# Strassen sums of an attention kernel moved to another place in VectorE's order

## The chip, the cores and the metric

The kernel runs on one core of a Trainium2 chip. A core has five engines that work side by side, each with its own queue of instructions taken in order: TensorE (PE, matmul), VectorE (DVE), ScalarE (ACT), GpSimd (POOL) and SyncE (SP), which here only issues DMAs. An instruction waits in its queue until the semaphores it needs have their values. The metric is the device time of one execution in microseconds (us). The kernel before has a median of 1221.35 us over 3 runs (1220.94 to 1221.71).

## The reference

Cut to what matters; x is 2048 x 512, 32 heads of width 128, a cache of 2048 keys and values per head, everything in bf16.

```python
xn = layernorm(x)
q  = heads(xn @ wq)                                  # wq 512 x 4096
p  = softmax(einsum("bhqd,bhkd->bhqk", q, k_cache) * Dh ** -0.5)
o  = einsum("bhqk,bhkd->bhqd", p, v_cache)
s  = merge(o) @ wo                                   # wo 4096 x 512
# the gate: a small MLP mixer of xn
h  = gelu(layernorm(xn) @ w1); h = shift_tokens(h)   # four column groups, by -1, +1, -2, +2
x1 = xn + h @ w2
g  = silu(x1 + gelu(layernorm(x1) @ w3) @ w4)
return x + s * g
```

## The kernel before, in words

**Units and slots.** The gate is computed first (about the first 190 us, overlapping the first attention units) and stored to DRAM. Attention is cut into 128 units: 8 groups of 4 heads (g), in each group 4 quarters of 512 tokens (qt), in each quarter the 4 heads (hh). So a group is 16 units. A unit has 8 slots, and the main loop runs over `n`, with `u, p = divmod(n, 8)`. In each slot TensorE computes scores of 256 keys by 512 tokens into PSUM (ps_s), ACT takes their exp into an SBUF tile (pT, L446, 128x1024), and TensorE multiplies the exp tiles of an earlier slot with the values (ps_o). Four pT tiles of 128x2048 make a unit.

**Softmax sums.** The exp tiles of a unit are added up into one tile, acc: `add_first` on DVE (L452, pT0 + pT1, recorded in slot 4), then pT2, whose lower half POOL adds and whose upper half DVE adds (`add_half`, L457, both 128x1024), then pT3 (`add_next`, L461), then two folds (L465, L469) down to 128x512. A DMA transposes it (tT), DVE reduces it (L499) and takes the reciprocal (L505), two DMAs spread it over the partitions (dr, rb), and `norm` (L523) multiplies ps_o with rb into oT.

**The q product.** For each pair of heads, q of 512 tokens is computed by a Strassen scheme with seven half-size products in place of eight. It needs sums of blocks of xn (`x_sum`, tiles xs, L366: four per quarter of tokens, made once) and of blocks of wq (`w_sum`, tiles wc, L375: four per pair of heads). The products' results are put together by ACT (`q_take`, L415) and DVE (`q_part`, L423, L426, L428, L431). The last of these additions, L431 (`qT<-ps_q,tq`, 128x512), is recorded in slot 6 of an odd unit, and the scores of the next unit, an even one, read what it writes.

**The wo product.** The same scheme for o @ wo, per group and quarter: sums of blocks of wo (`wo_sum`, tiles tw, L563, four per group; the third of most groups overwrites a block of wo itself), sums of blocks of oT (`o_sum`, tiles so, L572, four per quarter), seven products for each of two row blocks, and `wo_take` (L597), which adds the results into fp32 accumulators in SBUF (sacc). At the end the accumulators are joined, scaled by the gate and added to x.

**What sets the order.** Everything is written out by hand: dictionaries from a slot number to operations. `todo` (filled by `at`) runs at the end of a slot. `o_early` runs in slot 0, and in slot 4 just ahead of `add_first`. `o_steps` runs at the end of a slot, behind `q_part` of the same slot and ahead of `add_half`. As each engine takes its instructions in the order in which they are recorded, this fixes DVE's order. In an odd unit the order is: what `o_early` holds for slot 4, L452, L431, then L523, L499, L505, an L597, DVE's L457, L461 and the folds.

**Memory.** Pool `pS` (right side) opens when the gate's tiles are done and lies over their memory; it holds xs, wc, tw, so, sacc and others. Pool `pB` lies on the left side; `qtp` is a ring of 5 tiles for the queries of the first units, otherwise unused later on. A tile that lies over memory that was in use waits for the last instructions or DMAs that used it. The first tile of sacc is cleared in unit 8 by a memset on DVE (L545); the gate stores are DMAs on POOL's queue (L321).

Of the kernel before, what the change touches and what calls it, by code (L numbers as in the profile page):

```python
# [11 lines left out]
BF16 = mybir.dt.bfloat16  # L12
# [5 lines left out]
def kernel(  # L18
# [16 lines left out]
    P = nc.NUM_PARTITIONS  # L35
# [9 lines left out]
    QT = Sq // 512  # L45
# [5 lines left out]
    HG = 4  # L51
    NG = H // HG

    SPU = KC // 2
# [9 lines left out]
    def pool(name, bufs=1, space=None, **kw):  # L64
        if space is not None:
            kw["space"] = space
        return tc.tile_pool(name=name, bufs=bufs, **kw)
# [43 lines left out]
    def mm(out, lhsT, rhs, start, stop, **kw):  # L111
# [9 lines left out]
        out=ident[:], in0=diag[:], scalar1=0.0, scalar2=None, op0=ALU.is_equal))  # L121

    HEAD = 7
    XS = 3 * QT + 1
    TW = (2, 1, 0, 1)
    units = [(g, qt, hh) for g in range(NG) for qt in range(QT) for hh in range(HG)]
    LATE = (QT - 2, QT - 1)
# [7 lines left out]
    def at(n, fn):  # L135
        todo[n].append(fn)
# [209 lines left out]
    xs = {}  # L346
# [4 lines left out]
    def x_block(qt, half, dcs):  # L351
        c = qt * 512 + 256 * half
        return xnT[:, dcs, c:c + 256]

    def x_sum(qt, i):
        if i == 2 and qt < QT - 1:
            out = x_block(qt, 1, LO)
        else:
            out = pS.tile([P, 2, 256], BF16, tag="xs", bufs=XS, name="xs")[:]
        a, b, op = (  # L360
            (x_block(qt, 1, LO), x_block(qt, 1, HI), ALU.add),
            (xs.get((qt, 0)), x_block(qt, 0, LO), ALU.subtract),
            (x_block(qt, 0, LO), x_block(qt, 1, LO), ALU.subtract),
            (x_block(qt, 0, HI), xs.get((qt, 1)), ALU.subtract),
        )[i]
        pin(nc.vector.tensor_tensor(out=out, in0=a, in1=b, op=op))  # L366
        xs[qt, i] = out
# [185 lines left out]
    def wo_sum(g, i):  # L553
        w = wog[g]
        b11, b12, b21, b22 = (w[:, k, c] for k in (UP, DOWN) for c in (WL, WR))
        if i == 2 and g < NG - 2:
            out = b12
        elif i == 2:
            out = qtp.tile([P, 2, D // 2], BF16, tag="qT", bufs=5, name="tw")[:]
        else:  # L560
            out = pS.tile([P, 2, D // 2], BF16, tag=f"tw{i}", bufs=TW[i], name="tw")[:]
        a, b = ((b12, b11), (b22, tw.get((g, 0))), (b22, b12), (b21, tw.get((g, 1))))[i]
        pin(nc.vector.tensor_tensor(out=out, in0=a, in1=b, op=ALU.subtract))  # L563
        tw[g, i] = out
# [173 lines left out]
    def last_act(ts, cols):  # L738
        tb[ts, cols.start] = pS.tile([P, D // 2], BF16, tag="xs", bufs=XS, name="tb")
        pin(nc.scalar.activation(  # L740
            out=tb[ts, cols.start][:], in_=last_ps(ts, cols), func=ACT.Identity, scale=0.5))
# [245 lines left out]
    pB = left.enter_context(pool("pB", reuse_waits="tile"))  # L987
# [3 lines left out]
    pS = None  # L991
    for h in range(HG):
        load_wo(h)
    for g in range(NG - 1):
        b = (g * QT + QT - 1) * HG
        for hh in range(HG):
            h = (g + 1) * HG + hh
# [74 lines left out]
    o_steps, o_early = defaultdict(list), defaultdict(list)  # L1072
    for g, qt in BLOCK:
        u0 = ((g * QT + qt) * HG + 6) * SPU
        for i in range(2):
            a = u0 + 16 * i
            for k, n in ((1, 10), (7, 11), (2, 14), (4, 15), (6, 19), (5, 20), (3, 23)):
                steps[a + n].append((wo_product, g, qt, i, k))
            for k, n, which in ((7, 12, o_early), (4, 16, o_early), (5, 22, o_steps), (3, 24, o_early)):
                which[a + n].append((wo_take, g, qt, i, k))  # L1080
        for i, n, which in ((2, 3, o_steps), (0, 4, o_early), (1, 12, o_early), (3, 19, o_steps)):
            which[u0 + n].append((o_sum, g, qt, i))
    for g in range(NG - 1):
        u0 = ((g * QT + (g == 0)) * HG + 6) * SPU
        for i, n in ((0, -4), (2, -4 if g else 4), (1, 4), (3, 12)):
            o_early[u0 + n].append((wo_sum, g, i))
    for i, (qt, u) in enumerate((qt, qt * HG + 5 + j) for qt in range(1, QT) for j in range(2)):
        at(u * SPU + 6, lambda qt=qt, i=i: sa_clear(qt, i % 2))
    LATER = (BLOCK[-1][0] * QT + BLOCK[-1][1] + 1) * HG
# [2 lines left out]
    for i, u in enumerate((10, 11, 12, 13, 14, 16, 18, 20)):  # L1092
        n = (LATER + u) * SPU
# [24 lines left out]
        for fn, *args in plan.get(n, ()):  # L1118
            fn(*args)

    for j, u in enumerate((8, 8, 9, 9, 9, 9, 9, 11, 11, 13, 17, 17, 18, 19, 20, 20)):
        at(u * SPU + 3, lambda qt=(j // 4 - 1) % QT, i=j % 4: x_sum(qt, i))
    for h in range(2, H, 2):
        for i, u in enumerate((((-4, -3, -3, -3), (-1, -1, 0, 0))[h % HG // 2] if h >= HG else (8, 8, 9, 9))):
            o_early[(h // HG * QT * HG + u) * SPU + 4].append((w_sum, h, i))

    for v in range(1, NU):
        if v not in made and not FIRST <= v < LAST + 2:
# [3 lines left out]
    for n in range(UB * SPU):  # L1132
        u, p = divmod(n, SPU)
# [73 lines left out]
        if pS is None and not held:  # L1207
            right.close()
            pS = right.enter_context(pool("pS", side="right", reuse_waits="tile"))
# [3 lines left out]
    n = UB * SPU  # L1213
# [15 lines left out]
    def last_add(ts, cols, tm):  # L1229
        if cols.start == 0:  # L1230
            yl[ts] = pS.tile([P, D], BF16, tag="xs", bufs=XS, name="y")
        pin(nc.vector.tensor_tensor(out=yl[ts][:, cols], in0=tm, in1=sacc[t0 + ts][:, cols.start // (D // 2)], op=ALU.add))  # L1232
# [8 lines left out]
    def pv_to(k):  # L1241
# [29 lines left out]
        out=diag[:], in0=diag[:], scalar1=0.0, scalar2=None, op0=ALU.is_equal))  # L1271
# [98 lines left out]
```

## Time and profile before

| what | value |
|---|---|
| median of 3 runs | 1221.35 us |
| the profiled execution | 1223.05 us |
| its span | 1221.3 us |
| PE busy | 1215.1 us, 99% |
| DVE busy | 1090.0 us, 89% |
| ACT busy | 1107.5 us, 91% |
| POOL busy | 299.2 us, 24% |
| granted TensorE clock | full in all slices |

The profile is of one execution on the chip. Busy time counts instructions on an engine's datapath. A line such as `L457 POOL ... x117 | 248.7, 2125 | 725.8 <-DVE acc L452 403.1` is a group of instructions of one line of the kernel: 117 of them, 248.7 us in all, 2125 ns each in the mean, and POOL sat idle 725.8 us before them, 403.1 of it ended by DVE's L452. A timeline row gives the start, the duration and the operation, and in brackets the engine's idle time before it and what ended it. `out<-in` are the program's names for the tiles. Rows of instructions that follow one another on one engine overlap by some hundredths of a microsecond, since the next starts while the last is still draining.

### The profile page before, as it was taken

The page shows a single profiled execution, that of the slowest core. Times are in us where ns is not written, and L with a number is a line of the kernel's source. Part 1 is how long each engine was busy: PE and PEld are TensorE (multiplying, and loading weights), DVE is VectorE, ACT ScalarE, POOL GpSimd, SP SyncE. Part 2 cuts the span into 40 slices and gives each one's busy share as a digit, 9 for nine tenths or more (in the row PEclk, how much of TensorE's full clock was granted, in tenths as well). Part 3 has the DMA queues.
Part 4 walks back from the last instruction along what each step waited for, and adds up shares of the span by engine and source line. Part 5 has one row for each costly group of instructions (what it writes and reads, how often), then busy time and mean ns, then how long its engine had stood idle before and what let it go on. Part 6 is the DMA issues. An engine that isn't in the chain of part 4 may idle for free.

```text
span 1221.3 us, 18941 instructions
## 1 busy us (share of the span) xinstructions
PE 1215.1 (99%) x6657; PEld 673.7 (55%) x6657; DVE 1090.0 (89%) x1931; ACT 1107.5 (91%) x1243; POOL 299.2 (24%) x222
## 2 busy tenths in 40 slices
PE   9999999999999999999999999999999999999998
PEld 6466444555555555555555555555555555555555
DVE  7763779999999999999999899999999999989997
ACT  6345999999999999999999999999999999999996
POOL 5300001323222222222222222222222222233320
PEclk9999999999999999999999999999999999999999
DMA  7662323444444434445343433344434434356552
GB/s 178 167 153 61 57 57 83 96 88 95 74 90 89 100 65 91 84 99 89 70 95 86 102 69 85 90 96 78 85 85 91 100 66 93 86 102 109 123 113 66
DMA packets 248159, 113.07 MB, mean 93 GB/s; under 512 B 195328, under 2 KB 231296, under 8 KB 248064
## 3 DMA queue, kind: packets, MB, share of 16 engines
q1 hardware_dynamic: 244560, 107.21, 41.4%
q0 software_dynamic: 2944, 4.20, 1.5%
q8 instruction: 52, 0.85, 0.3%
q14 instruction: 43, 0.35, 0.2%
q10 hardware_dynamic: 560, 0.46, 0.1%
HBM read 69.60 MB, written 4.45 MB: 61 GB/s over the span
## 4 chain that ended last, share of the span: by engine, by line
PE 96%; DVE 2%; ACT 1%; DMA 0%; issue 0%; DVEq 0%; ACTq 0%
PE ps_s L112 40%; PE ps_o L112 37%; PE ps_q L112 8%; PE ps_wo L112 8%; PE ps_m L112 3%; ACT pT L446 1%; DVE acc L461 0%; PE ps_warm L112 0%; DMA tT<-acc 0%; DVE acc L452 0%; DVE sacc L597 0%; PE ps_oh L112 0%; DVE y L1232 0%; DVE sm L499 0%; DVE acc L457 0%
## 5 line engine op out<-in xcount | busy, mean ns | idle before, releaser
L446 ACT ACTIVATE pT<-ps_s 128x1024 bf16<-128x1024 f32 x1016 | 1016.6, 1028 | 44.6 <-PE ps_s L112 12.8
L112 PE MATMUL ps_s<-qT,kT 128*128 128x512 bf16 (+1 forms) x2064 | 609.2, 377 | 1.5 <-ACT pT L446 0.9
L112 PE MATMUL ps_o<-pT,vb 128*128 128x512 bf16 x1984 | 589.9, 379 | 0.0
L457 POOL TENSOR_TENSOR acc<-acc,pT 128x1024 bf16<-128x1024 bf16 x117 | 248.7, 2125 | 725.8 <-DVE acc L452 403.1
L112 PEld LDWEIGHTS <-vb 128*128 128x128 bf16 x1984 | 194.0, 98 | 216.6
L112 PEld LDWEIGHTS <-kT 128*128 128x128 bf16 x2064 | 230.8, 113 | 73.7 <-DVE qT L431 3.0
L461 DVE TENSOR_TENSOR acc<-acc,pT 128x2048 bf16<-128x2048 bf16 x137 | 167.7, 1224 | 20.9 <-ACT pT L446 5.1
L452 DVE TENSOR_TENSOR acc<-pT 128x2048 bf16<-128x2048 bf16 x127 | 154.8, 1219 | 11.3 <-ACT pT L446 11.3
L597 DVE TENSOR_TENSOR sacc<-ps_wo,sacc 128x512 f32<-128x512 f32 x200 | 121.8, 609 | 3.0 <-PE ps_wo L112 1.7
L523 DVE TENSOR_TENSOR oT<-ps_o,rb 128x512 bf16<-128x512 f32 x127 | 86.6, 682 | 7.3 <-DMA rb<-dr 7.1
L465 DVE TENSOR_TENSOR acc<-acc 128x1024 bf16<-128x1024 bf16 x127 | 87.3, 687 | 2.4
L499 DVE TENSOR_REDUCE sm<-tT 128x4 f32<-128x512 bf16 x124 | 83.9, 677 | 5.8 <-DMA tT<-acc 5.5
L457 DVE TENSOR_TENSOR acc<-acc,pT 128x1024 bf16<-128x1024 bf16 x117 | 80.6, 688 | 0.0
L112 PEld LDWEIGHTS <-wc 128*128 128x128 bf16 x448 | 43.8, 98 | 52.9 <-issue 0.2
L112 PE MATMUL ps_wo<-wo_h,oT 128*128 128x256 bf16 (+1 forms) x296 | 71.1, 307 | 0.0
L112 PEld LDWEIGHTS <-oT 128*128 128x128 bf16 x428 | 41.6, 98 | 45.6
L112 PEld LDWEIGHTS <-so 128*128 128x128 bf16 x400 | 39.1, 98 | 47.2
L112 PEld LDWEIGHTS <-wq_h 128*128 128x128 bf16 x396 | 38.7, 98 | 46.1
L112 PE MATMUL ps_q<-xnT,wq_h 128*128 128x256 bf16 (+1 forms) x284 | 58.8, 295 | 0.0
L301 ACT ACTIVATE h2T<-ps_s 128x1024 bf16<-128x1024 f32 x28 | 28.6, 1023 | 31.6 <-PE ps_s L112 31.6
L469 DVE TENSOR_TENSOR acc<-acc 128x512 bf16<-128x512 bf16 x127 | 53.4, 420 | 2.4
L112 PEld LDWEIGHTS <-w_sb 128*128 128x128 bf16 x368 | 33.6, 98 | 29.2 <-issue 0.2
(134 smaller groups left out, 926.4 us busy)
## 6 DMA issues: line engine op xcount, KB each, us to landing
rb<-dr SPq DMA_DIRECT2D x127, 256.0 KB, 3.9
vb<-in_A_v_cache_dram SPq DMA_DIRECT2D x62, 256.0 KB, 3.0
wq_h<-in_A_wq_dram SPq DMA_DIRECT2D x32, 128.0 KB, 2.5
wo_h<-in_A_wo_dram SPq DMA_DIRECT2D x32, 128.0 KB, 2.4
w_sb<-in_B_w_dram SPq DMA_DIRECT2D x8, 256.0 KB, 5.0
kT<-in_A_k_cache_dram SPq DMA_TRANSPOSE x128, 2.7
gate<-xall POOLq DMA_DIRECT2D x16, 128.0 KB, 2.2
sacc<-in_A_x_dram POOLq DMA_DIRECT2D x8, 256.0 KB, 4.6
```

The costliest lines, as they stand in the source:

```text
L112: pin(nc.tensor.matmul(out=out, lhsT=lhsT, rhs=rhs, start=start, stop=stop, **kw))
L301: pin(nc.scalar.activation(out=h2[c][:, f], in_=ps[:], func=ACT.Gelu_apprx_tanh))
L446: pin(nc.scalar.activation(out=s["pT"][-1][:, jj:jj + 2, :], in_=sps[:], func=ACT.Exp, scale=SCALE))
L452: pin(nc.vector.tensor_tensor(out=s["acc"][:], in0=s["pT"][0][:], in1=s["pT"][1][:], op=ALU.add))
L457: pin(eng.tensor_tensor(out=a[:, part, :], in0=a[:, part, :], in1=e[:, part, :], op=ALU.add))
L461: pin(nc.vector.tensor_tensor(out=a[:], in0=a[:], in1=st[u]["pT"][i][:], op=ALU.add))
L465: pin(nc.vector.tensor_tensor(out=a[:, 0:2, :], in0=a[:, 0:2, :], in1=a[:, 2:4, :], op=ALU.add))
L469: pin(nc.vector.tensor_tensor(out=a[:, 0, :], in0=a[:, 0, :], in1=a[:, 1, :], op=ALU.add))
L499: pin(nc.vector.tensor_reduce(out=sm[:], in_=s["tT"][:], axis=mybir.AxisListType.X, op=ALU.add))
L523: pin(nc.vector.tensor_tensor(out=to, in0=o, in1=rb, op=ALU.mult))
L597: pin(nc.vector.tensor_tensor(out=out, in0=ps, in1=out, op=ALU.add))
```

## The change

It touches where sums of the two Strassen schemes are recorded, and in which pool a few of their tiles lie. The number of operations is the same (1526 tensor-tensor operations on DVE), and the orders on TensorE, ACT, POOL and SP are the same; only DVE's order differs.

- **Token sums (`x_sum`).** The sixteen move from units 8 to 20 to units 2 to 11. Tiles of the quarters 0 and 3 come from the left pool (tag "xe", 7 tiles), those of quarters 1 and 2 from pS as before (6 instead of 13 tiles).
- **`o_sum` number 1** moves from slot 4 of an odd unit, ahead of L452, to slot 6 of that unit, behind L431.
- **Weight sums of wo (`wo_sum`).** From group 1 on, numbers 1 and 3 take their tiles from the ring `qtp`, and the four are spread over three or four units; those in odd units stand in slot 6, behind L431, those in even units in slot 4, ahead of L452.
- **Weight sums of wq (`w_sum`).** From head 4 on, spread over units -4, -4, -3, -3 or -2, -1, 0, 0 before their group; those in odd units stand in slot 6, behind L431.

In the new DVE order 49 of the 56 L431 have one to three of these sums directly behind them; before, none had.

```diff
-    XS = 3 * QT + 1
+    XE, XS = 7, 3 * (QT - 2)
...
-            out = pS.tile([P, 2, 256], BF16, tag="xs", bufs=XS, name="xs")[:]
+            pl, tag, n = (pS, "xs", XS) if 0 < qt < QT - 1 else (pB, "xe", XE)
+            out = pl.tile([P, 2, 256], BF16, tag=tag, bufs=n, name="xs")[:]
...
-        elif i == 2:
+        elif i == 2 or i % 2 and g:
             out = qtp.tile([P, 2, D // 2], BF16, tag="qT", bufs=5, name="tw")[:]
...
-        for i, n, which in ((2, 3, o_steps), (0, 4, o_early), (1, 12, o_early), (3, 19, o_steps)):
+        for i, n, which in ((2, 3, o_steps), (0, 4, o_early), (1, 14, o_steps), (3, 19, o_steps)):
             which[u0 + n].append((o_sum, g, qt, i))
+    WSUMS = [[(i, 8 * u + (4, 6)[u % 2]) for i, u in us] for us in (
+        ((0, -5), (1, -3), (2, -2), (3, -1)), ((0, -13), (1, -5), (2, -2), (3, -1)))]
     for g in range(NG - 1):
         u0 = ((g * QT + (g == 0)) * HG + 6) * SPU
-        for i, n in ((0, -4), (2, -4 if g else 4), (1, 4), (3, 12)):
-            o_early[u0 + n].append((wo_sum, g, i))
+        for i, n in ((0, -4), (2, -4 if g else 4), (1, 4), (3, 12)) if g == 0 else WSUMS[g > 1]:
+            (o_early if n % 8 == 4 else o_steps)[u0 + n].append((wo_sum, g, i))
...
-    for j, u in enumerate((8, 8, 9, 9, 9, 9, 9, 11, 11, 13, 17, 17, 18, 19, 20, 20)):
+    for j, u in enumerate((2, 2, 3, 4, 4, 5, 5, 6, 8, 8, 9, 9, 9, 9, 11, 11)):
         at(u * SPU + 3, lambda qt=(j // 4 - 1) % QT, i=j % 4: x_sum(qt, i))
     for h in range(2, H, 2):
-        for i, u in enumerate((((-4, -3, -3, -3), (-1, -1, 0, 0))[h % HG // 2] if h >= HG else (8, 8, 9, 9))):
-            o_early[(h // HG * QT * HG + u) * SPU + 4].append((w_sum, h, i))
+        for i, u in enumerate((((-4, -4, -3, -3), (-2, -1, 0, 0))[h % HG // 2] if h >= HG else (8, 8, 9, 9))):
+            plan, p = (o_steps, 6) if h >= HG and u % 2 else (o_early, 4)
+            plan[(h // HG * QT * HG + u) * SPU + p].append((w_sum, h, i))
```

## The prediction

> **What bounds the kernel now.** I read the page first: busy shares, the chain, the costliest groups.
>
> ```profile
> PE 1215.1 (99%) x6657; PEld 673.7 (55%) x6657; DVE 1090.0 (89%) x1931; ACT 1107.5 (91%) x1243; POOL 299.2 (24%) x222
> ...
> PE 96%; DVE 2%; ACT 1%; DMA 0%; issue 0%; DVEq 0%; ACTq 0%
> ...
> L457 POOL TENSOR_TENSOR acc<-acc,pT 128x1024 bf16<-128x1024 bf16 x117 | 248.7, 2125 | 725.8 <-DVE acc L452 403.1
> ```
>
> TensorE sets the end. VectorE is 89% busy over the whole span, but that is an average over stages, so I asked for windows next: first the stretch that holds units 2 to 6, then one over units 12 to 110, where attention, the q product and the wo product run together.
>
> ```profile
> 100.00:200.00 100.00, 100.00 (x480) 48.99 (x479) 67.13 (x100) 85.37 (x93) 7.97 (x13) 1.00 0.29 61
> ...
> 225.27:1062.31 837.04, 835.50 (x4554) 467.24 (x4553) 785.09 (x1381) 808.76 (x893) 216.10 (x104) 1.00 0.41 87
> ```
>
> The columns are PE, weight loads, DVE, ACT, POOL. In the second stretch DVE is busy 785.09 of 837.04 us: it has 51.95 us left in 99 units (99 L452 below), about half a microsecond each, and TensorE is full. A kernel like this turns DVE-bound as soon as each unit costs DVE a little more, so the whole question is what the moved operations cost DVE in their new place. The groups of that stretch:
>
> ```profile
> L452 DVE TENSOR_TENSOR acc<-pT 128x2048 bf16<-128x2048 bf16 x99 | 120.6, 1218 | 0.2 <-ACT pT L446 0.2
> L523 DVE TENSOR_TENSOR oT<-ps_o,rb 128x512 bf16<-128x512 f32 x100 | 68.2, 682 | 5.9 <-DMA rb<-dr 5.9
> L499 DVE TENSOR_REDUCE sm<-tT 128x4 f32<-128x512 bf16 x100 | 67.7, 677 | 5.7 <-DMA tT<-acc 5.5
> L572 DVE TENSOR_TENSOR so<-oT 128x512 bf16<-128x512 bf16 x48 | 20.1, 422 | 12.9 <-PE ps_wo L112 12.8
> L375 DVE TENSOR_TENSOR wc<-wq_h,wc 128x256 bf16<-128x256 bf16 x26 | 7.4, 285 | 0.2
> L563 DVE TENSOR_TENSOR tw<-wo_h,tw 128x512 bf16<-128x512 bf16 x12 | 5.0, 419 | 0.0
> ```
>
> Where TensorE itself waits, I read its timeline:
>
> ```profile
> 259.85 0.62 PE L112 MATMUL ps_s<-qT,kT 128*128 128x512 bf16 x2 [0.68 <-DVE qT L431]
> ...
> 327.94 0.62 PE L112 MATMUL ps_s<-qT,kT 128*128 128x512 bf16 x2 [0.41 <-ACT pT L446]
> ...
> 868.50 0.62 PE L112 MATMUL ps_s<-qT,kT 128*128 128x512 bf16 x2 [0.45 <-ACT pT L446]
> ```
>
> These are the starts of units 16, 24 and 88, each behind the query's last addition (L431) of the unit before; the idle column adds to 0.68 + 0.41 + 0.45 = 1.54 us. Matmuls overlap, so counted from start to start against the usual 216 ns these three are 0.84, 0.58 and 0.61 us late; that is 2.0 us, and with 0.1 at unit 120 I put what can be won there at 2.1 us.
>
> **The change, part by part.** One odd unit of before, DVE in order, and below it POOL's operation of the same unit:
>
> ```profile
> 375.46 0.28 DVE L375 TENSOR_TENSOR wc<-wq_h,wc 128x256 bf16<-128x256 bf16 x1
> 375.66 1.22 DVE L452 TENSOR_TENSOR acc<-pT 128x2048 bf16<-128x2048 bf16 x1
> 376.80 0.68 DVE L431 TENSOR_TENSOR qT<-ps_q,tq 128x512 bf16<-128x512 f32 x1
> 377.40 0.68 DVE L523 TENSOR_TENSOR oT<-ps_o,rb 128x512 bf16<-128x512 f32 x1
> 378.00 0.68 DVE L499 TENSOR_REDUCE sm<-tT 128x4 f32<-128x512 bf16 x1
> 378.71 0.18 DVE L505 RECIPROCAL rc<-sm 128x4 f32<-128x4 f32 x1
> 378.80 0.67 DVE L597 TENSOR_TENSOR sacc<-ps_wo,sacc 128x512 f32<-128x512 f32 x1
> 379.39 0.68 DVE L457 TENSOR_TENSOR acc<-acc,pT 128x1024 bf16<-128x1024 bf16 x1
> 380.20 1.23 DVE L461 TENSOR_TENSOR acc<-acc,pT 128x2048 bf16<-128x2048 bf16 x1
> ```
>
> ```profile
> 377.02 2.13 POOL L457 TENSOR_TENSOR acc<-acc,pT 128x1024 bf16<-128x1024 bf16 x1 [7.06 <-ACT pT L446]
> ```
>
> *Sums behind L431.* In the changed program's DVE order, 49 of the 56 L431 have one to three of the moved sums directly behind them; in the old one none has. Their number and sizes stay, so their own busy time (0.285 to 0.422 us each) only changes place. Ahead of L452 goes what now stands behind L431, which lets L431 end earlier by 0.2 to 0.6 us in these units: the 2.1 us above would go. What would be late next is L523, hence the wo product that reads oT.
>
> But look at what they meet. POOL's half of the exp sum starts 0.14 us after L452 ends (376.88 to 377.02) and runs 2.13 us. A sum that starts where L523 stood (377.40) falls 0.38 us into it. Between 377.02 and 379.15 DVE executes only operations with one input in SBUF: L431, L523 and L597 take the other from PSUM, L499 and L505 have one. The moved sums read both inputs from SBUF, as does DVE's L457, which starts 0.24 us after POOL is done. In this stretch no such sum starts early in POOL's add, so the price must come from the few places where L457 starts before POOL's end, a DVE row and POOL's row each:
>
> ```profile
> 1133.33 0.90 DVE L457 TENSOR_TENSOR acc<-acc,pT 128x1024 bf16<-128x1024 bf16 x1
> ```
>
> ```profile
> 1131.56 2.12 POOL L457 TENSOR_TENSOR acc<-acc,pT 128x1024 bf16<-128x1024 bf16 x1 [6.84 <-DVE acc L452]
> ```
>
> ```profile
> 522.72 0.87 DVE L457 TENSOR_TENSOR acc<-acc,pT 128x1024 bf16<-128x1024 bf16 x1
> ```
>
> ```profile
> 520.92 2.13 POOL L457 TENSOR_TENSOR acc<-acc,pT 128x1024 bf16<-128x1024 bf16 x1 [6.81 <-ACT qT L415]
> ```
>
> Here L457 starts 0.35 and 0.33 us before POOL ends (1133.68, 523.05), takes 0.90 and 0.87 in place of 0.68, and ends 0.55 and 0.54 us after POOL's end. POOL's time is unchanged. So of 0.34 us of overlap 0.21 is lost, and the end hangs on POOL's. I read that as: the operation waits for POOL's instruction to be over, and 0.13 us of start-up passes meanwhile. The low bound is the loss seen, 0.21 us a sum; the high one a wait for POOL's end. I take the high one, since the end follows POOL's to 0.01 us.
>
> The Trainium skill, SBUF — State Buffer, section "Who interferes with whom", says the same without a limit of length: a DVE instruction with two SBUF inputs contends with a GpSimd instruction that reads SBUF, and the later one is blocked until the earlier is finished. The rows of this case agree for the last 0.34 us of POOL's 2.13; no run here shows it for the first. By that rule the loss is the 1.6 us worked out next, by the bare row 49 x 0.21 = 10.3 us in all.
>
> With the wait a first sum of 128x512 (0.42 us, of which 0.13 start-up) ends at 379.15 + 0.29 = 379.44, and L523 starts by 379.36 at the soonest (operations overlap by 0.08) against 377.40 + 0.34 = 377.74 without contention: 1.6 us of DVE lost. A second or third sum of the same unit starts after POOL's end and loses nothing. 49 x 1.61 = 78.9 us of DVE time.
>
> *What DVE can absorb.* Of its 51.95 idle us, part lies between operations that read each other's result: 380.20 against 380.07, and 0.03 three times, 0.22 a unit, 99 x 0.22 = 21.8. That stays. The other 30.2 us can be used up. Of these L523 and L499 wait 5.9 + 5.5 = 11.4 for DMAs that DVE's own earlier work releases; 15 of those 19 waits, with 8.6 us, lie in places a unit's length from the moved sums, as the first and the last of them show (L431 of the first one's unit is at 259.11):
>
> ```profile
> 250.47 0.69 DVE L523 TENSOR_TENSOR oT<-ps_o,rb 128x512 bf16<-128x512 f32 x1 [0.78 <-DMA rb<-dr]
> ...
> 909.38 0.69 DVE L523 TENSOR_TENSOR oT<-ps_o,rb 128x512 bf16<-128x512 f32 x1 [0.53 <-DMA rb<-dr]
> ```
>
> I leave these 8.6 standing. 78.9 - 30.2 + 8.6 = 57.3 us that DVE falls behind, and TensorE, which needs its qT, oT and emptied accumulators, with it. The ends: 78.9 - 30.2 = 48.7 if all idle time is used, 78.9 if none is. The 2.1 us of TensorE's old waits are inside this, since DVE then sets the pace.
>
> *Token sums in units 2 to 6.* Eight x_sum go where DVE is 67% busy; they cost nothing there (if they did, L452 of those units would wait and its exp tiles come free late: 8 x 0.34 = 2.7 us at most). Six leave units 13 to 20, at the start-to-start time of two in a row:
>
> ```profile
> 204.84 0.42 DVE L366 TENSOR_TENSOR xs<-xnT,xs 128x512 bf16<-128x512 bf16 x1
> 205.18 0.42 DVE L366 TENSOR_TENSOR xs<-xnT 128x512 bf16<-128x512 bf16 x1
> ```
>
> 6 x 0.34 = 2.0 us won if DVE sets the pace there.
>
> *Moved tiles.* Seven xs tiles go to the left pool, two kinds of tw to the query's ring, so the right pool shrinks and its tiles lie elsewhere over the memory it takes over. In the built program the first sacc memset (L545) then also waits for the last gate store, which itself waits for the L318 just ahead:
>
> ```profile
> 194.41 0.69 DVE L318 SCALAR_TENSOR_TENSOR xall<-th,xall 128x512 bf16<-128x512 bf16 x1
> 195.10 0.27 DVE L545 MEMSET sacc<- 128x256 f32 x1
> 195.29 0.63 DVE L656 COPY sacc<-ps_wo 128x512 f32<-128x512 f32 x1
> ```
>
> ```profile
> 195.40 0.54 POOL L321 DMA_DIRECT2D gate<-xall  x1 [12.28 <-DVE sacc L545]
> ```
>
> ```profile
> DMA to landing us min/median/max: 2.0/2.2/3.9
> ```
>
> That store (issues of L321, the last line) goes out at 195.40 and lands 2.0 to 3.9 us later, 2.3 for this one: the memset starts near 197.7, 2.6 us late. Behind it on DVE stand the copy that empties ps_wo, the first x and weight sums and L452, and TensorE waits for the emptied ps_wo and exp tiles. DVE has hardly any idle time in the units just after; from the slack that its later operations have I put what reaches TensorE at 2.1 us, with 0 and 3 as ends. POOL's memsets change what they wait for too, with nothing near behind them; the SP queue's order is the same.
>
> The sum: 57.3 - 2.0 + 2.1 = 57.4 us. On the profiled execution (1223.05 us: span 1221.3 and 1.75 around it) that makes 1280.5; it is 1.7 above the median of the runs, 1221.35, so I forecast 1278.8 for the median. What a measurement can tell from no change is about 0.2%, 2.4 us.
>
> **The rivals.**
> *A. POOL and DVE share, and DVE is only slowed.* The 0.34 us of overlap brought 0.13 us of progress; read as a speed of 0.38, a 0.42 us sum takes 1.1 us, 0.6 more. 49 x 0.6 = 29 us against 30 of idle time: about 1222, or some 8 us more where the 8.6 isn't usable, 1230. The constant end speaks against it, but both overlaps are of one length, so it isn't excluded.
> *B. No contention worth speaking of.* The waits of 2.1 us go, the memset costs 2.1: 1221.4. Against it stand the four rows above.
> *C. The other side: L431 comes earlier at no price, and the memset's wait is covered.* Then TensorE loses its waits at units 16, 24 and 88 and nothing comes back: 1221.35 - 2.1 = 1219.2, or 1218.5 if the small waits of unit 120 and a few more go too, just outside what can be told. It decides if the sums run in POOL's add at 0.42 us and if the store lands before 195.5. The 0.90 and the 2.0 us speak against it.
> *D. Nothing of the idle time is recovered,* because DVE, now late, waits for the DMAs and exp results that come later still: 1221.35 + 78.9 = 1300. The window's 51.95 us speak against: much of it ends by TensorE's work (L572's 12.9), which would be long done.
>
> **How the numbers follow.** Blocked until POOL's end, 0.77 (own range 1268 to 1294); A 0.08; B 0.07; C 0.04; D 0.04. The likeliest gives 1279. The range 1245 to 1298 leaves out B, C, most of A and half of D. Faster by over 0.2% needs C's better end, 0.03; within 0.2%: B, the rest of C, and a third of A, 0.11; slower, 0.86.
>
> **What would show it.** The sums of so, tw and wc in odd units take 1.5 to 2.1 us where they stand first behind L431 and keep 0.28 to 0.42 elsewhere; each ends 0.2 to 0.3 us after POOL's add. L523 follows 1.6 us later than now. A pair of units, 16.87 us (837.04 over 49.6 pairs), grows by about 1.0 to 1.2. PE gets waits on DVE all through the stretch from unit 12, its weight loads and ACT sink in share with it, DVE's busy share rises to 97% or more, and DVE idle by PE's ps_wo goes. The first memset starts near 197.7. Before 195 us nothing moves but the eight L366. I am wrong if the sums keep 0.42 us inside POOL's add, if POOL starts later than now (its add released by something other than L452, so that a sum slips in ahead and POOL is the one that waits), or if the pair's length doesn't grow.

## The result and the profile after

The changed kernel takes 1269.18 us in the median of 5 runs (1268.12 to 1270.73), the kernel before 1221.6 us beside it. The ratio is 1.0392, with a 95% interval of 1.0377 to 1.0407: 47.6 us slower. The profiled execution took 1269.18 us, its span is 1267.3. Line numbers are one higher than before in most of the file (L431 is L432, L452 is L453, L457 is L458, L523 is L524, L572 is L573).

The page of the changed kernel, its busy shares, its chain and POOL's add:

```profile
PE 1219.0 (96%) x6534; PEld 673.9 (53%) x6657; DVE 1160.6 (92%) x1931; ACT 1110.6 (88%) x1243; POOL 299.0 (24%) x222
...
DVE 60%; PE 25%; issue 11%; DMA 2%; ACT 1%; DVEq 0%; POOL 0%; SPq 0%; POOLq 0%; ACTq 0%
...
L458 POOL TENSOR_TENSOR acc<-acc,pT 128x1024 bf16<-128x1024 bf16 x117 | 248.6, 2125 | 772.0 <-DVE acc L453 373.4
```

TensorE held 96% of the chain before; now DVE holds 60%. DVE's busy time rose by 70.6 us, though it executes the same 1931 instructions. POOL's add takes 2125 ns as before. An odd unit shows where the time sits; DVE first, POOL's add below:

```profile
384.63 1.22 DVE L453 TENSOR_TENSOR acc<-pT 128x2048 bf16<-128x2048 bf16 x1
385.76 0.68 DVE L432 TENSOR_TENSOR qT<-ps_q,tq 128x512 bf16<-128x512 f32 x1
386.36 1.89 DVE L376 TENSOR_TENSOR wc<-wq_h 128x256 bf16<-128x256 bf16 x1
388.17 0.28 DVE L376 TENSOR_TENSOR wc<-wq_h,wc 128x256 bf16<-128x256 bf16 x1
388.38 0.68 DVE L524 TENSOR_TENSOR oT<-ps_o,rb 128x512 bf16<-128x512 f32 x1
...
389.77 0.66 DVE L598 TENSOR_TENSOR sacc<-ps_wo,sacc 128x512 f32<-128x512 f32 x1
```

```profile
385.98 2.12 POOL L458 TENSOR_TENSOR acc<-acc,pT 128x1024 bf16<-128x1024 bf16 x1 [5.73 <-ACT pT L447]
```

Two sums of one size and one kind stand behind L432. The first starts 0.38 us into POOL's add and takes 1.89 us; it ends 0.15 us after POOL (388.25 against 388.10). The second takes 0.28. In the profile this wait is no idle time and has no releaser: it shows only as a longer instruction. The groups over units 12 to 110 show it for all kinds (mean ns is the number behind the comma):

```profile
L573 DVE TENSOR_TENSOR so<-so,oT 128x512 bf16<-128x512 bf16 x24 | 48.4, 2015 | 0.0
L564 DVE TENSOR_TENSOR tw<-wo_h,tw 128x512 bf16<-128x512 bf16 x12 | 22.6, 1887 | 0.0
...
L573 DVE TENSOR_TENSOR so<-oT 128x512 bf16<-128x512 bf16 x48 | 18.1, 418 | 0.0
L524 DVE TENSOR_TENSOR oT<-ps_o,rb 128x512 bf16<-128x512 f32 x99 | 67.3, 680 | 0.3 <-DMA rb<-dr 0.3
L500 DVE TENSOR_REDUCE sm<-tT 128x4 f32<-128x512 bf16 x99 | 66.7, 674 | 5.7 <-DMA tT<-acc 5.6
```

The 24 `so<-so,oT` are the moved ones and take 2.0 us instead of 0.42; the 48 `so<-oT`, which stayed, take 0.42. The 49 sums that stand first behind L432 together take 77.7 us more than their own time. Who waits for whom on TensorE, from 190 us on:

```profile
PE ps_wo L112 <- DVE sacc L598: 30.3, 49, 1.4
PE ps_q L112 <- DVE tq L424: 4.2, 8, 0.6
PE ps_wo L112 <- DVE sacc L657: 2.4, 1, 2.4
```

TensorE does not wait for the sums that are held up. It waits 49 times, about once a pair of units, for wo_take (L598, the last row of the unit above), which stands behind them on DVE and empties ps_wo. The stretch from the exp that opens unit 12 to the one that opens unit 112, before and after (us, then PE, weight loads, DVE, ACT, POOL):

```profile
225.95:1071.74 845.79, 844.25 (x4598) 471.85 (x4597) 792.57 (x1394) 816.84 (x900) 218.20 (x105) 1.00 0.41 87
```

```profile
228.33:1117.98 889.65, 849.98 (x4509) 471.63 (x4597) 860.87 (x1386) 820.18 (x901) 218.64 (x105) 1.00 0.39 82
```

It grew by 43.9 us: DVE's busy time by 68.3, while its idle time fell from 53.2 to 28.8. The other step is in unit 8, the memset:

```profile
194.24 0.68 DVE L318 SCALAR_TENSOR_TENSOR xall<-th,xall 128x512 bf16<-128x512 bf16 x1
198.93 0.27 DVE L546 MEMSET sacc<- 128x256 f32 x1 [4.01 <-DMA gate<-xall]
```

```profile
199.80 0.59 PE L112 MATMUL ps_wo<-wo_h,oT 128*128 128x512 bf16 x2 [2.37 <-DVE sacc L657]
```

DVE stands still for 4.01 us until the gate store has landed, and TensorE loses 2.4 to 2.5. The exps up to unit 8 keep their spacing to 0.01 us, so the eight token sums of units 2 to 6 cost nothing. 2.5 + 43.9 = 46.4 us; the spans differ by 46.0.

### The profile page after: what moved, and what is told of

It is laid out like the page before. It is cut to its first block, busy times and chain, and to the rows that moved or that the text cites. A ratio compares the mean times of both kernels' runs of the same rounds, so it can differ in the third digit from the quotient of the medians.

```text
span 1267.3 us, 18834 instructions
## 1 busy us (share of the span) xinstructions
PE 1219.0 (96%) x6534; PEld 673.9 (53%) x6657; DVE 1160.6 (92%) x1931; ACT 1110.6 (88%) x1243; POOL 299.0 (24%) x222
## 4 chain that ended last, share of the span: by engine, by line
DVE 60%; PE 25%; issue 11%; DMA 2%; ACT 1%; DVEq 0%; POOL 0%; SPq 0%; POOLq 0%; ACTq 0%
PE ps_s L112 11%; DVE acc L462 9%; PE ps_o L112 9%; DVE acc L453 8%; DVE sacc L598 7%; DVE acc L458 4%; DVE sm L500 4%; DVE so L573 4%; DVE oT L524 4%; DVE acc L470 3%; DVE tw L564 3%; DVE acc L466 2%; DVE qT L432 2%; PE ps_q L112 2%; PE ps_wo L112 2%
## 5 line engine op out<-in xcount | busy, mean ns | idle before, releaser
L112 PE MATMUL ps_o<-pT,vb 128*128 128x512 bf16 x1884 | 568.3, 379 | 4.7
L458 POOL TENSOR_TENSOR acc<-acc,pT 128x1024 bf16<-128x1024 bf16 x117 | 248.6, 2125 | 772.0 <-DVE acc L453 373.4
L462 DVE TENSOR_TENSOR acc<-acc,pT 128x2048 bf16<-128x2048 bf16 x137 | 167.7, 1224 | 20.9 <-ACT pT L447 5.1
L453 DVE TENSOR_TENSOR acc<-pT 128x2048 bf16<-128x2048 bf16 x127 | 154.6, 1217 | 8.2 <-ACT pT L447 8.2
L598 DVE TENSOR_TENSOR sacc<-ps_wo,sacc 128x512 f32<-128x512 f32 x200 | 121.0, 605 | 0.0
L500 DVE TENSOR_REDUCE sm<-tT 128x4 f32<-128x512 bf16 x124 | 83.6, 674 | 5.7 <-DMA tT<-acc 5.6
L524 DVE TENSOR_TENSOR oT<-ps_o,rb 128x512 bf16<-128x512 f32 x127 | 86.4, 680 | 1.3 <-DMA rb<-dr 0.8
L458 DVE TENSOR_TENSOR acc<-acc,pT 128x1024 bf16<-128x1024 bf16 x117 | 80.5, 688 | 0.0
L112 PE MATMUL ps_wo<-wo_h,so 128*128 128x256 bf16 x192 | 36.5, 271 | 30.3 <-DVE sacc L598 30.3
```

The costliest lines, as they stand in the source:

```text
L112: pin(nc.tensor.matmul(out=out, lhsT=lhsT, rhs=rhs, start=start, stop=stop, **kw))
L453: pin(nc.vector.tensor_tensor(out=s["acc"][:], in0=s["pT"][0][:], in1=s["pT"][1][:], op=ALU.add))
L458: pin(eng.tensor_tensor(out=a[:, part, :], in0=a[:, part, :], in1=e[:, part, :], op=ALU.add))
L462: pin(nc.vector.tensor_tensor(out=a[:], in0=a[:], in1=st[u]["pT"][i][:], op=ALU.add))
L500: pin(nc.vector.tensor_reduce(out=sm[:], in_=s["tT"][:], axis=mybir.AxisListType.X, op=ALU.add))
L524: pin(nc.vector.tensor_tensor(out=to, in0=o, in1=rb, op=ALU.mult))
```

## The experiments

The theory (P): a DVE operation that reads both inputs from SBUF and starts while POOL's add runs waits until that is over. Rivals: the moved tiles or the chosen units make the loss (T), DVE's new order alone makes it (O), POOL and DVE share and DVE is slowed. The kernel before had medians of 1221.34, 1221.63 and 1221.45 us beside the three sets of runs. The edits are shown by the parts of lines that change, against the changed kernel unless the text says otherwise.

**ahead.** The same sums in the same units, but ahead of L453.

```diff
-(1, 14, o_steps)
+(1, 12, o_early)
-(o_early if n % 8 == 4 else o_steps)[u0 + n].append((wo_sum, g, i))
+o_early[u0 + n // 8 * 8 + 4].append((wo_sum, g, i))
-plan, p = (o_steps, 6) if h >= HG and u % 2 else (o_early, 4)
+plan, p = o_early, 4
```

> The changed kernel with its sums of odd units put back ahead of the first sum of exp tiles (L453), in the same units; the tiles and the token sums stay moved. Theory P (a sum with two SBUF inputs waits until POOL's add is over): nothing starts in POOL's add any more, the sums take 0.42 and 0.28 us, and what remains over the kernel before is the late memset of unit 8, 2.5 us: 1223 to 1225. Rival T (the loss comes from the moved tiles, the ring of query tiles above all, or from the units chosen): it stays, 1260 to 1270.

Measured: 1224.72 us, ratio 1.0031 (1.002 to 1.0042), as P has it. Two groups of it:

```profile
L573 DVE TENSOR_TENSOR so<-so,oT 128x512 bf16<-128x512 bf16 x24 | 9.9, 414 | 0.0
L564 DVE TENSOR_TENSOR tw<-wo_h,tw 128x512 bf16<-128x512 bf16 x12 | 5.0, 414 | 0.0
```

The place of the sums is worth 44.5 us; tiles, units and number of sums are the same as in the changed kernel. T falls.

**nopool.** The changed kernel without POOL's add.

```diff
-            add_half(u, nc.gpsimd, LO) if u in APART else add_next(u, 2)
+            if u not in APART:
+                add_next(u, 2)
```

> The changed kernel without POOL's add: the lower half of the third exp tile is left out of the softmax sums of nearly all units, all else is kept, the sums stand behind L432. P: the sums take 0.42 and 0.28 us there, 1221 to 1225. Rival O (DVE's new order alone makes it late, POOL has no part): 1260 to 1270.

Measured: 1224.88 us, ratio 1.0031 (1.0019 to 1.0043). DVE's order is that of the changed kernel, and the sums behind L432 run in their own time:

```profile
L573 DVE TENSOR_TENSOR so<-so,oT 128x512 bf16<-128x512 bf16 x24 | 9.9, 414 | 0.0
L564 DVE TENSOR_TENSOR tw<-wo_h,tw 128x512 bf16<-128x512 bf16 x12 | 5.0, 414 | 0.0
```

O falls: without POOL the order costs nothing.

**poolwrites.** POOL is as busy as before, but reads nothing from SBUF.

```diff
-            add_half(u, nc.gpsimd, LO) if u in APART else add_next(u, 2)
+            if u in APART:
+                for _ in range(2):
+                    pin(nc.gpsimd.memset(st[u]["acc"][:, LO, :], 0.0))
+            else:
+                add_next(u, 2)
```

> The changed kernel with POOL's add replaced by two memsets of the same half of acc, which write and read nothing (so the lower halves of the first three exp tiles are lost from the softmax sums); they wait for L453 as the add did and fill about 1.9 us. If only an instruction of POOL that reads SBUF holds the sums up: 0.42 and 0.28 us, 1221 to 1225. If any instruction of POOL does: sums of about 1.6 us, 1255 to 1265.

Measured: 1224.92 us, ratio 1.0026 (1.0014 to 1.0037). DVE behind L453, and POOL's two memsets of the same unit (one row, x2):

```profile
379.25 0.69 DVE L432 TENSOR_TENSOR qT<-ps_q,tq 128x512 bf16<-128x512 f32 x1 [0.34 <-PE ps_q L112]
379.86 0.28 DVE L376 TENSOR_TENSOR wc<-wq_h 128x256 bf16<-128x256 bf16 x1
380.06 0.29 DVE L376 TENSOR_TENSOR wc<-wq_h,wc 128x256 bf16<-128x256 bf16 x1
380.26 0.68 DVE L524 TENSOR_TENSOR oT<-ps_o,rb 128x512 bf16<-128x512 f32 x1
```

```profile
378.97 1.96 POOL L1208 MEMSET acc<- 128x1024 bf16 x2 [6.21 <-DVE acc L453]
```

Both sums lie wholly inside POOL's 378.97 to 380.93 and take 0.28 us. In other units a sum of 128x512 lies wholly inside one of the two memsets, 0.46 us into its 0.95, and takes 0.42. POOL being busy holds nothing up; POOL's add does. The two differ in what they read, and also in the operation, so that it is the reading is the simplest account, not the only one.

**quarter.** POOL's add half as long.

```diff
-            add_half(u, nc.gpsimd, LO) if u in APART else add_next(u, 2)
+            add_half(u, nc.gpsimd, slice(0, 1)) if u in APART else add_next(u, 2)
```

> The changed kernel with POOL's add cut to its first half (128x512), the other half of it left out of the softmax sums; all else is kept. If a sum waits for the end of POOL's instruction: POOL takes about 1.1 us, a sum behind L432 starts 0.38 us into it, waits 0.7 and ends 0.29 us behind POOL, so it takes 1.0 us, 0.58 over its own time. 49 x 0.58 = 28 us against 31 of usable idle time in DVE: most of the 45 us are gone, 1225 to 1235. If the cost is one per encounter, whatever POOL's length: sums of 1.9 us and 1269.

Measured: 1231.69 us, ratio 1.008 (1.0066 to 1.0094). DVE and POOL in one odd unit:

```profile
380.24 0.69 DVE L432 TENSOR_TENSOR qT<-ps_q,tq 128x512 bf16<-128x512 f32 x1
380.85 0.99 DVE L376 TENSOR_TENSOR wc<-wq_h 128x256 bf16<-128x256 bf16 x1
```

```profile
380.54 1.16 POOL L458 TENSOR_TENSOR acc<-acc,pT 128x512 bf16<-128x512 bf16 x1 [6.70 <-DVE acc L453]
```

The sum ends 0.14 us after POOL again (381.84 against 381.70). 48 sums are held up, 32.7 us in all instead of 77.7, and the time lies in the range expected for a wait until POOL's end. POOL's time went from 2.13 to 1.16 us, and the loss per sum from 1.59 to 0.68: 0.91 us for 0.97. The wait lasts as long as POOL's instruction does. A mere slowing of DVE would not end at POOL's end in both kernels.

**between.** The sums stand between L453 and L432, so that they start before POOL's add does. (`o_late` is a new dictionary, run in slot 4 behind `add_first`.)

```diff
-(1, 14, o_steps)
+(1, 12, o_late)
-(o_early if n % 8 == 4 else o_steps)[u0 + n].append((wo_sum, g, i))
+(o_early[u0 + n] if n % 8 == 4 else o_late[u0 + n - 2]).append((wo_sum, g, i))
-plan, p = (o_steps, 6) if h >= HG and u % 2 else (o_early, 4)
+plan, p = (o_late, 4) if h >= HG and u % 2 else (o_early, 4)
             add_first(u)
+            run_all(o_late, n)
```

> The changed kernel with its sums of odd units between L453 and L432, so that DVE starts them 0.08 us before L453 ends, ahead of POOL's add, which is released by L453. If the first to start holds what both need: the sum takes 0.42 us, POOL's add starts or ends about 0.3 us later, DVE loses nothing, 1223 to 1225. If POOL's add goes ahead whatever the order: 1.9 us a sum as before, 1265 to 1270.

Measured: 1235.14 us, ratio 1.0111 (1.0096 to 1.0127), neither of the two. A unit with two sums of different kinds, DVE and POOL:

```profile
397.39 1.21 DVE L453 TENSOR_TENSOR acc<-pT 128x2048 bf16<-128x2048 bf16 x1
398.52 0.42 DVE L573 TENSOR_TENSOR so<-so,oT 128x512 bf16<-128x512 bf16 x1
398.86 2.21 DVE L376 TENSOR_TENSOR wc<-wq_h,wc 128x256 bf16<-128x256 bf16 x1
400.99 0.68 DVE L432 TENSOR_TENSOR qT<-ps_q,tq 128x512 bf16<-128x512 f32 x1
```

```profile
398.74 2.18 POOL L458 TENSOR_TENSOR acc<-acc,pT 128x1024 bf16<-128x1024 bf16 x1 [5.73 <-ACT pT L447]
```

The first sum starts 0.22 us ahead of POOL, takes its 0.42 us, and POOL's row is 2.18 long instead of 2.13. The second starts 0.12 us behind POOL and takes 2.21. This happened in 7 units, wherever a second sum came after POOL's start. There L432 is late and the next unit's scores with it:

```profile
PE ps_s L112 <- DVE qT L432: 8.8, 7, 1.4
```

So the order of starting decides which engine waits. The seven second sums cost TensorE 8.8 us of waiting between them. That the first ones, ahead of POOL, cost nothing is shown by single_nt below.

**only_so.** The kernel before with one of the moves.

```diff
-for i, n, which in ((2, 3, o_steps), (0, 4, o_early), (1, 12, o_early), (3, 19, o_steps)):
+for i, n, which in ((2, 3, o_steps), (0, 4, o_early), (1, 14, o_steps), (3, 19, o_steps)):
```

> The kernel before with one part of the change, o_sum number 1 behind L431: 25 sums that wait 1.6 us, 40 us of DVE, in every other pair of units. DVE's usable idle time is 0.63 us a pair. If a lag is made up in the pair that follows: 25 x (1.6 - 2 x 0.63) = +9 us, 1230, and up to 1236 where a pair has less to give. If nothing is made up between them: 25 x (1.6 - 0.63) = +24, 1246. If the harm needs several sums together: 1222.

Measured: 1238.44 us, ratio 1.0139 (1.0125 to 1.0153). The moved sums and the stretch of units 12 to 111:

```profile
L572 DVE TENSOR_TENSOR so<-so,oT 128x512 bf16<-128x512 bf16 x24 | 47.2, 1965 | 0.0
```

```profile
225.87:1087.03 861.16, 844.85 (x4509) 471.57 (x4597) 825.64 (x1394) 818.75 (x900) 217.89 (x105) 1.00 0.40 85
```

24 sums lose 37.1 us; the stretch grew by 861.16 - 845.79 = 15.4. So 21.7 us were absorbed, 0.90 a sum, between the 0.63 us of one pair and the 1.26 of two. The likely reading is that the pair without a moved sum makes up some of the lag, but not all that its idle time would allow. My 1230 to 1236 was too low, 1246 too high.

**later.** The sums in the next slot 0, behind DVE's own half, when POOL is done. (`o_late` runs there behind L462 in this kernel.)

```diff
-(1, 14, o_steps)
+(1, 16, o_late)
-(o_early if n % 8 == 4 else o_steps)[u0 + n].append((wo_sum, g, i))
+(o_early[u0 + n] if n % 8 == 4 else o_late[u0 + n + 2]).append((wo_sum, g, i))
-plan, p = (o_steps, 6) if h >= HG and u % 2 else (o_early, 4)
+plan, p = (o_late, 8) if h >= HG and u % 2 else (o_early, 4)
```

> The changed kernel with its sums of odd units moved on into the next slot 0, behind DVE's own half (L458) and L462, when POOL's add is over. P: 0.42 and 0.28 us each; L432 is still early, so TensorE's waits at units 16, 24 and 88 (2.1 us) are gone, and the memset's 2.5 us stay: about 1222. O or T: 1260 to 1270.

Measured: 1229.86 us, ratio 1.0072 (1.0056 to 1.0087): the loss is mostly gone, as P has it, but 1222 was wrong by 8. TensorE's waits from 225 us on:

```profile
PE ps_q L112 <- DVE wc L376: 3.1, 6, 0.7
PE ps_wo L112 <- DVE so L573: 2.4, 3, 1.5
```

In this place the sums are late for their own products. 5.5 us of new waits took the place of the old.

**later_nt.** The same place, on the kernel before: without moved token sums and without their tiles, so that the first memset doesn't wait for the gate store. The edit is against later; the line of `x_sum` that takes the tile goes back too.

```diff
-    XE, XS = 7, 3 * (QT - 2)
+    XS = 3 * QT + 1
-(2, 2, 3, 4, 4, 5, 5, 6, 8, 8, 9, 9, 9, 9, 11, 11)
+(8, 8, 9, 9, 9, 9, 9, 11, 11, 13, 17, 17, 18, 19, 20, 20)
```

> The kernel before with only the weight sums and o_sum number 1 moved, and these into the next slot 0, behind DVE's own half and L461; the token sums and their tiles stay, and the memset has nothing to wait for. P: TensorE's waits at units 16, 24 and 88 go, 2.1 us: 1219.5. If another wait takes their place: 1221.6.

Measured: 1227.21 us, ratio 1.0046 (1.0034 to 1.0059). The waits for wc and so are there again (2.6 and 1.2 us), and the time is above both values expected. It is 2.65 us less than later: the moved tiles and token sums.

**tokens** and **tiles.** The kernel before with the first part of the change alone, and with its tiles alone. tokens has all three edits, tiles the first two:

```diff
-    XS = 3 * QT + 1
+    XE, XS = 7, 3 * (QT - 2)
...
-            out = pS.tile([P, 2, 256], BF16, tag="xs", bufs=XS, name="xs")[:]
+            pl, tag, n = (pS, "xs", XS) if 0 < qt < QT - 1 else (pB, "xe", XE)
+            out = pl.tile([P, 2, 256], BF16, tag=tag, bufs=n, name="xs")[:]
...
-(8, 8, 9, 9, 9, 9, 9, 11, 11, 13, 17, 17, 18, 19, 20, 20)
+(2, 2, 3, 4, 4, 5, 5, 6, 8, 8, 9, 9, 9, 9, 11, 11)
```

> The kernel before with the token sums alone moved to units 2 to 11 and their tiles as in the changed kernel. The memset waits for the last gate store: +2.5 us, 1224.1. If the sums that leave units 13 to 20 bring something, up to 0.8 us less (the wait at unit 16): 1223.3. If the eight sums of units 2 to 6 cost TensorE anything, more than 1224.5.

> The kernel before with the tiles of the token sums moved as in the changed kernel, and the token sums where they were. If the 3.2 us of the kernel with the token sums moved are the memset's wait for the last gate store: 1224.5. If the token sums' new units cost part of it: less, down to 1222.

Measured: tokens 1224.56 us, ratio 1.0024 (1.0013 to 1.0035); tiles 1226.11 us, ratio 1.0035 (1.0023 to 1.0047). The memset of tiles:

```profile
198.92 0.27 DVE L546 MEMSET sacc<- 128x256 f32 x1 [3.88 <-DMA gate<-xall]
```

The tiles alone cost 4.7 us, above both values expected, and tokens 3.2. In both profiles the exps of units 0 to 8 keep their times and unit 9 is about 4 us late; in the changed kernel it is 2.5 us late at the same wait of DVE. The difference is the clock of TensorE behind that wait. The stretch from 200 to 204 us, in the changed kernel and in tiles (the last numbers are the granted clock, the DMA share and GB/s):

```profile
200.00:204.00 4.00, 3.95 (x19) 1.99 (x19) 3.93 (x9) 2.87 (x4) 1.67 (x1) 1.00 0.12 33
```

```profile
200.00:204.00 4.00, 4.00 (x11) 1.45 (x11) 3.93 (x9) 1.02 (x1) 1.49 (x1) 0.57 0.14 35
```

In tiles 8 matmuls follow one another at about 427 ns instead of 216, which makes 1.7 us; tokens (clock 0.59) and poolwrites (0.61) show the same. In the profiles of after, ahead, nopool, quarter, between and later the clock stays at 1.00 behind the same wait, so what lowers it is open. The 1.5 us between the medians of tiles and tokens is of the size of this loss; that the new places of the token sums give anything back isn't shown.

**ahead_nt** and **single_nt.** Two tries for a version that keeps what could be won: the token sums and their tiles as in the kernel before, the weight sums spread as in the change, all sums ahead of L452 (ahead_nt), or one sum of an odd unit between L452 and L431 and the rest ahead (single_nt). To the edits of later_nt come those of ahead, or those of between and

```diff
+    for n in list(o_late):
+        o_early[n] += o_late[n][:-1]
+        o_late[n] = o_late[n][-1:]
```

> The kernel before with only the weight sums spread over more units (and their tiles in the query's ring), all ahead of L452; token sums, their tiles and o_sum as before. Without the memset's wait: at best the waits of 16, 24 and 88 go, 1219.5; if those were of one execution, 1221.5.

> As the last, but one sum of each odd unit stands between L452 and L431, and a second or third one ahead of L452. If the 13 us of the kernel with all sums between came from the seven second sums that started behind POOL: no sum is blocked, 1219.5 to 1221.5. If standing between the two costs TensorE by the later L431 anyway: 1225 or more.

Measured: ahead_nt 1221.88 us, ratio 1.0000 (0.9992 to 1.0009); single_nt 1221.82 us, ratio 0.9999 (0.999 to 1.0008). single_nt, a moved kind on DVE and POOL's add:

```profile
L572 DVE TENSOR_TENSOR so<-so,oT 128x512 bf16<-128x512 bf16 x24 | 10.0, 418 | 0.0
```

```profile
L457 POOL TENSOR_TENSOR acc<-acc,pT 128x1024 bf16<-128x1024 bf16 x100 | 215.0, 2150 | 623.4 <-DVE acc L452 448.7 <-ACT pT L446 135.8 <-DMA tT<-acc 27.0
```

One sum just ahead of POOL's add costs nothing. What the seven second sums of between had cost is gone. But neither version gains, as the second value of each expectation has it: these two places have nothing to win.

## Why the prediction was right

The forecast was 1278.8 us, the range 1245 to 1298; measured were 1269.2, at the low edge of the 1268 to 1294 that the blocked case had of its own. The case was the one forecast, and its mechanism is shown: nopool, ahead, poolwrites, quarter and between each take away or change one condition of it, and the time follows.

- **The wait.** 49 x 1.61 = 78.9 us predicted, 77.7 measured. The rows of before allowed 0.21 us a sum or 1.6; the choice of the high end, because the operation ended 0.54 and 0.55 us after POOL's end, holds. The 128x512 sums end 0.28 to 0.29 us after POOL, the prediction had 0.29; those of 128x256 end 0.15 after, outside the 0.2 to 0.3 named.
- **The Trainium skill's rule** (SBUF — State Buffer, "Who interferes with whom"): the later of the two is blocked until the earlier is finished. The rows now show it from 0.12 us into POOL's add on (between: 2.21 us), and for two lengths of the add. The trace also agrees on the order (in between POOL's row, the later one, grows by 0.05 us for 0.20 of overlap with a sum and by 0.13 for 0.27) and on a GpSimd instruction that only writes (poolwrites: sums of 0.28 and 0.42 us beside a memset).
- **What DVE can absorb** is the term that was mis-sized, and it makes up most of the difference. Predicted for the stretch were +55.3 us (78.9 - 30.2 + 8.6 - 2.0), measured are +43.9. The wait itself accounts for 1.2 of these 11.4 us. The idle time fell by 24.4 us where 30.2 - 8.6 = 21.6 was predicted, 2.8 more: 28.8 were left, 5.9 of them before L500 and L524, where 8.6 were left standing. The other 7.4: DVE's busy time rose by only 68.3, where 77.7 less 2.0 for the token sums would make 75.7. Some 4.6 of them are the overlap of 0.08 us between an operation and the one before it, which an operation behind a gap doesn't have: when the gaps of before close, each gives back 0.08 beside its length. In the two stretches 959 operations overlap with the one before them in the kernel before and 1016 in the changed one, 78.7 and 83.3 us in all. The prediction left this out. Another 0.9 is the token sums: the prediction counted six that leave units 13 to 20, the list in the diff has seven, with 2.9 us of rows. L598 ran 0.8 us less in all, and the rest, about 1, is rows at the ends of the stretches.
- **The memset.** The wait is there as described; 4.0 us on DVE instead of 2.6, since the store took 3.5 us to land instead of 2.3. On TensorE 2.5 against 2.1.
- **Token sums in units 2 to 6** cost nothing, as forecast.
- **The 2.1 us of TensorE's waits** at units 16, 24 and 88, which rival C hoped for, were mostly those of one execution: that profile took 1.7 us more than the median. ahead_nt spreads the sums, and its median is that of before. C had no gain to make.
- **The signs.** The pair of units went from 16.92 to 17.79 us (845.79 and 889.65 over 50), +0.88 where 1.0 to 1.2 was named; DVE is busy 860.87 of 889.65 us, 96.8% where 97% or more was named. Rival A (sharing) falls with the 2.0 us sums, where it had 1.1, and with quarter, B (no contention) with the same 2.0 us, D with DVE's lost idle time.

The trace of before could already have ruled out rival A, since it has L457 at shorter overlaps too. Here it starts 0.18 us before POOL's end and loses 0.04:

```profile
218.55 0.72 DVE L457 TENSOR_TENSOR acc<-acc,pT 128x1024 bf16<-128x1024 bf16 x1
```

```profile
216.61 2.12 POOL L457 TENSOR_TENSOR acc<-acc,pT 128x1024 bf16<-128x1024 bf16 x1 [4.98 <-ACT pT L446]
```

Of 0.11 us of overlap (at 1062.85) nothing is lost, of 0.18 0.04, of 0.34 0.20. That is the overlap less 0.14, and nothing where the overlap is shorter, as a wait for POOL's end with a start-up of 0.14 makes it. A speed of 0.38 would lose 0.07, 0.11 and 0.21.

## What to carry to other kernels

An operation has a price that depends on what runs beside it, and a profile shows that price as a longer instruction, not as a wait. Before a DVE operation with two SBUF inputs is moved, look at whether POOL is then reading SBUF; right ahead of POOL's start it cost nothing here, right behind it all that POOL had left. And where a stretch has a second engine at 94%, the question to a change is what it adds to that engine, counted against its usable idle time.

## What the runs showed of the hardware

- An operation that waits for POOL's add does its start-up meanwhile: 128x256 ends 0.15 us after POOL, 128x512 0.28 to 0.29, against 0.28 and 0.42 us alone. So about 0.14 us of it pass while it waits.
- The reverse wait is cheap here: a sum that started 0.22 us ahead of POOL's add made POOL's row 0.05 us longer (2.18 against 2.13), though the two overlapped by 0.20 us. Two sums of 128x256 in a row, with 0.27 us left at POOL's start, made it 0.13 longer (2.26). Both are about the overlap less 0.14, as if POOL too did a start-up while it waited.
- Two POOL memsets of 128x1024 bf16 (1.96 us) let two-input sums through at full speed; one add of the same size (2.13 us) let through none of the 49 that started behind it in the changed kernel.
- A 128 KB store on POOL's queue, whose row is 0.54 us long, held DVE for 4.0 us: it landed 3.5 us after it went out.
- Behind the stop of 2.1 to 2.4 us that this made TensorE take, the granted clock was 0.57 to 0.61 from 200 to 204 us in three profiles (tiles, tokens, poolwrites) and 1.00 in six others.
